# A chained attention, dense MoE and soft MoE kernel: w1 loads on a second queue, later combine steps, working tiles as stream slots, sums turned by pairs

## The chip, the cores and the metric

One core of a Trainium2 chip runs the whole program. The metric is device time in microseconds (us). TensorE is called PE, VectorE DVE, ScalarE ACT, GpSimd POOL, SyncE SP; "idle" of an engine is time between its instructions.

## The reference

Three stages, all float32, with B=4 batches, H=8 heads, S=576, D=64, so N=2304 rows of DM=512:

```
p_packed = softmax(p k^T / 8) v              # 32 packed rows for each head
x   = softmax(q p_packed^T / 8) p_packed     # attention output, 2304 x 512
P   = domain_probs / sum                     # 4 dense experts, F = 1024
x   = sum_e P[:, e] * (relu(x @ w1[e]) @ w2[e])
logits = x @ phi                             # 8 soft experts, 4 slots each: 32 columns
slot_in  = softmax(logits over rows).T @ x   # 32 x 512
slot_out = per expert e: relu(slot_in[e] @ m1[e]) @ m2[e]
out = softmax(logits over columns) @ slot_out
```

w1 and w2 are those of the dense MoE, m1 and m2 those of the soft one (8 x 512 x 1024 and 8 x 1024 x 512).

## The kernel before, in words

**Order of work.** Python emits every engine's instructions in a fixed order, and each engine runs its own list in that order, waiting on semaphores. A head computes attention for batch 0 under a small planner (`place_ops`). Then a loop runs over 128 slots, 32 for each batch. Slot s does `flip_h(s-1)` (a DVE transpose of the hidden block into the ring `hr`), `mm1(s)` (12 matmuls, hidden rows = g x a, L620; ACT, POOL and every fourth half DVE finish them, L630, L631, L625), at every fourth slot `make_g` for the next four slots (L585, L595, L597) and `logits` (L653), and then whatever is due in that slot.

**w1.** `make_g(ci)` multiplies a 1 MB block of w1 by the packed rows. There is one w1 tile, so the load of block ci+1 is issued at the end of `make_g(ci)`, on SP's queue, in SP's list behind all loads emitted before it.

**wphi.** In the head and batch 0 w2 is multiplied by phi (`wphi_ops`): for each of 8 blocks, four PE turns (L260) with ACT copies (L267), a projection (L275), an ACT copy `pick` (L286), a PE turn `back` (L291), an ACT copy `keep` (L294).

**Soft MoE in the loop.** While batch b+1 runs, `softmaxes(b)` is stepped from slots 0 to 3 and at `C_AT`. The latter are the column softmax, here called the combine steps: den and cm (DVE, L735 to L743), a POOL subtraction (L745), an ACT exp (L749), a sum and reciprocal (DVE, L751 to L753), a POOL product (L755), a turn into `cts` (DVE, L758). `pooling(b)` (L775) adds into `tacc`. The attention of the next batch is emitted one stage per slot for group 0 from slot 8 and group 1 from slot 12 (`ATT_AT`); stage 0 turns k (L344), 2 is sa (L358), 3 the maximum (L382), 5 the normalization (L408 to L413), 6 the PE turn `et` (L419), 8 pv (L455), 9 the packing into pkn (L468, L471), 10 sb (L358), 11 nat (L500, L506), 14 the sum (L520), 17 the split of a2 into two parts: `hi` on ACT (L537), `lo` on POOL (L542).

**The stream.** From the last batch on, 80 chunks of 512 KB (16 of w2, 32 of m1, 32 of m2) are loaded on SP in order of use into slots. A slot is a piece of SBUF that has come free: 8 of a pool, 2 of a2, 4 of a ring place, 2 of w1, 4 of g, 2 of a2, 1 of wphi, and 16 of four ring places that become free block by block as the last `pooling` reads them: 39. Chunk 39 goes where chunk 0 was, once that is used. (L849 issues.)

**The end.** After slot 127: last logits, softmax over rows, `pooling` (L775), sums into `tacc` (L789), all remaining combine steps, then 16 turns of `tacc` through `fold` (tt, L1133) with two copies, `si` (L1148, chunks 0 to 15), its turn `sit`, `hid` (L1196, chunks 16 to 47), `so` (L1242, chunks 48 to 79). m2 is taken by four experts at a time: experts 0 to 3 in full width (512), then experts 4 to 7 in two parts of 256 columns, so 16 chunks are in parts. After a part its columns are summed (`sr`, L1259), multiplied by `ct` (o, L1273), copied by ACT and DVE (L1233) and stored (L1280), all before the next part's so on PE.

Of the kernel before, what the change touches and what calls it, by code (L numbers as in the profile page):

```python
# [18 lines left out]
def tile_packed_attention_moe_softmoe(  # L19
# [40 lines left out]
    ATT_AT = (8, 12)  # L60
    C_AT = (8, 9, 10, 11, 12, 13)
# [12 lines left out]
    soft = main.enter_context(tc.tile_pool(name="soft", bufs=1))  # L74
# [39 lines left out]
    flat = [hr[:, i].rearrange("p a b -> p (a b)") for i in range(RING)]  # L114
    m_run = const.tile([128, NB], F32, name="m_run")
# [84 lines left out]
    class Op:  # L200
        def __init__(self, stage, eng, cost, fn, deps, take=0, give=0, rank=0):
# [47 lines left out]
    def wphi_ops(n, loaded, next_load):  # L249
# [48 lines left out]

        puts = []
        for x in range(4):  # L300
            ops.append(Op(0, "PE", 0.47, lambda x=x: turn(x), [loaded], take=1, rank=2))
            ops.append(Op(0, "ACT", 0.58, lambda x=x: put(x), [ops[-1]], give=1, rank=2))
            puts.append(ops[-1])
        ops.append(Op(0, "PE", 1.3, project, puts, take=1, rank=2))
        if next_load:
            next_load.deps.append(ops[-1])
            ops.append(next_load)
        pr = [o for o in ops if o.fn is project]
        ops.append(Op(0, "ACT", 0.27, pick, pr, give=1, rank=2))
        ops.append(Op(0, "PE", 0.15, back, ops[-1:], take=1, rank=2))  # L310
        ops.append(Op(0, "ACT", 0.27, keep, ops[-1:], give=1, rank=2))
# [14 lines left out]
    def attention(b, g, tmp, late, gp, loads=None):  # L326
# [219 lines left out]
    def att_tmp(tag, name):  # L546
        if tag == "a2":
            return sw("t0", name)
# [117 lines left out]
    def sw(tag, name):  # L666
        return soft.tile([128, S], F32, tag=tag, name=name)

    def spread_p(n):

        t = sw("t0", f"ps{n}").rearrange("p (x s) -> p x s", s=32)
# [3 lines left out]
        pe_t[n] = soft.tile([128, S], F32, tag="pe", name=f"pe{n}", bufs=2)  # L675
# [6 lines left out]
    def softmaxes(b, halves=False):  # L682
        la = sw("la", f"la{b}")
# [23 lines left out]
        d = sw("t2", f"d{b}").rearrange("p (x s) -> p x s", s=32)  # L707
# [14 lines left out]
        lt = sw("t1", f"lt{b}").rearrange("p (x s) -> p x s", s=32)  # L722
# [79 lines left out]
    so_steps = [(s, 0, DM) for s in range(NX // 4 - 1)]  # L802
    so_steps += [(NX // 4 - 1, d0, dw) for d0, dw in parts]
# [10 lines left out]
    for s, d0, dw in so_steps:  # L814
        nx = CHUNK // dw
        for x in range(0, NFT, nx):
            for e in range(4):
                chunks.append(
                    m2[4 * s + e, 512 * (x // 4) : 512 * (x // 4) + 512, d0 : d0 + dw].rearrange(
                        "(p x) d -> p x d", x=4  # L820
                    )[:, x % 4 : x % 4 + nx]
                )
# [59 lines left out]
    with tc.manual_schedule():  # L882
# [89 lines left out]
        for n in range(NCH):  # L972
# [7 lines left out]
            ops += wphi_ops(n, landed[n], after)  # L980
            ops.append(Op(0, "NONE", 0.0, done, ops[-1:], rank=2))
        rest = place_ops(ops)
# [57 lines left out]
        for s in range(nslot):  # L1040
# [35 lines left out]
            elif last == SPB - 3:  # L1076
                add_slots(2, w1_place)
            if last >= 0:
# [31 lines left out]
        fin = ctx.enter_context(tc.tile_pool(name="fin", bufs=1, reuse_waits="tile"))  # L1110
        tt = fin.tile([128, 2, NFT, 64], F32, tag="tt", name="tt")
        ct = fin.tile([128, NB // 2, XR, 2, 2, 32], F32, name="ct")
        rr_t = fin.tile([128, DM], F32, name="rr")
# [4 lines left out]
        hm = [fin.tile([128, NFT, 4, 32], F32, name=f"hm{s}") for s in range(2)]  # L1118
        sel = fin.tile([128, 128], F32, name="sel")
        si = leftover(0, DM)  # L1120

        for c in range(4):
            for s in range(2):
                pool.tensor_copy(
                    sel[:, 32 * c + 16 * s : 32 * c + 16 * s + 16].rearrange(
                        "p (x s) -> p x s", x=4
                    ),
                    ident.rearrange("p (x r) -> p x r", x=4)[:, :, 4 * s : 4 * s + 4],
                )
# [12 lines left out]
        ck = 0
        ps = mm_ps("si")
        for x in range(0, NFT, 2):
            cks = [chunk_t.pop(ck + e) for e in range(NE)]
            for xl in range(2):
                for e in range(NE):
                    pe.matmul(  # L1148
                        ps[32 * e : 32 * e + 32, :],
                        tt[:, e % 2, x + xl, 32 * (e // 2) : 32 * (e // 2) + 32],  # L1150
# [22 lines left out]
        for s in range(2):  # L1173
            pool.memset(hm[s], 0.0)
        for s in range(2):
            for dc in range(NDC):
# [5 lines left out]
                )  # L1182

# [23 lines left out]
        hid = fin.tile([128, DF], F32, tag="tt", name="hid")  # L1207
        act.activation(out=hid[:, :512], in_=hp[0], func=AF.Relu)
        dve.tensor_scalar_max(hid[:, 512:], hp[1], 0.0)
        for i in range(2):  # L1210
# [5 lines left out]
            for s in range(2):  # L1216
                (act.copy if i else dve.tensor_copy)(
                    hm[s][:, 4 * i : 4 * i + 4, :, 4 * s : 4 * s + 4].rearrange(
                        "p a b c -> p (a b) c"
                    ),  # L1220
                    ps.rearrange("p (a c) -> p a c", c=32)[:, :, 4 * s : 4 * s + 4],
# [92 lines left out]
```

## Time and profile before

| | us |
|---|---|
| median of 3 runs (lowest, highest) | 508.59 (506.87, 512.04) |
| the profiled execution, its own time | 507.49 |
| its span, first to last instruction | 505.7 |
| PE busy, DVE busy, POOL busy, ACT busy | 472.3, 290.9, 204.4, 181.7 |

The profile is one execution. Its time is its span and 1.8 us around it. Times in the rows count from the span's start. By stage: head to about 58 us, batches 0 to 3 of the loop to about 406 us, the end to 505.7 us. An engine's busy share says little by itself: what counts is what ends last in each stage.

### The profile page before, as it was taken

Reading aid. Unit: us, or ns where it says so; the run is one execution under the profiler, and the core shown is the slowest. Engines: PE = TensorE matmul, PEld = TensorE weight load, DVE = VectorE, ACT = ScalarE, POOL = GpSimd, SP = SyncE. Lnnn points to the kernel's source line nnn. Section 1 sums busy time; section 2 is a strip of 40 time slices with the busy share of each in tenths; the row PEclk is TensorE's granted clock in tenths of the full one; section 3 lists DMA queues with packets and bytes.
Section 4 is the critical chain, followed back from the end, with each engine's and each line's share of the span. In section 5 each row is a group of like instructions: output and inputs, shape, how many; then the busy total and the mean of one; then the engine's idle time right before and its main releaser. Section 6 shows DMA issues by size and latency. Waiting matters only on the chain.

```text
span 505.7 us, 13249 instructions
## 1 busy us (share of the span) xinstructions
PE 472.3 (93%) x5608; PEld 334.9 (66%) x5608; DVE 290.9 (58%) x551; ACT 181.7 (36%) x449; POOL 204.4 (40%) x266
## 2 busy tenths in 40 slices
PE   6899799999999989999998999999999998998695
PEld 3767677778775767778566678775787866322153
DVE  3683355687781777886559588781875545100022
ACT  2475455435440434354224335440434310200033
POOL 3024233357942544586326157941656513100000
PEclk9999999999999999999999899999999997899986
DMA  8989832457231447643215243285672479999997
GB/s 197 382 311 272 298 130 81 135 136 232 84 123 47 131 141 178 177 143 112 86 68 194 71 128 103 86 294 207 244 256 85 166 275 403 414 412 412 383 383 273
DMA packets 57740, 104.36 MB, mean 206 GB/s; under 512 B 5904, under 2 KB 24848, under 8 KB 57680
## 3 DMA queue, kind: packets, MB, share of 16 engines
q1 hardware_dynamic: 57552, 103.36, 59.6%
q8 instruction: 44, 0.72, 0.6%
q0 software_dynamic: 128, 0.15, 0.3%
q14 instruction: 16, 0.13, 0.1%
HBM read 98.78 MB, written 4.72 MB: 205 GB/s over the span
## 4 chain that ended last, share of the span: by engine, by line
PE 77%; DMA 12%; DVE 6%; SPq 3%; ACT 1%; issue 1%; ACTq 0%; DVEq 0%
PE h L620 39%; PE pb L775 8%; PE lg L653 7%; PE g L585 6%; DMA ck<-in_moe_w_dram 4%; DMA hr<-in_moe_w_dram 4%; DMA w<-in_moe_w_dram 4%; PE pv L455 3%; PE sa L358 2%; PE o L1273 2%; SPq L849 2%; PE w2t L260 2%; PE sb L358 2%; PE et L419 1%; PE tt L1133 1%; PE so L1242 1%
## 5 line engine op out<-in xcount | busy, mean ns | idle before, releaser
L631 POOL TENSOR_TENSOR ht<-ht,pe 128x288 f32<-128x288 f32 x192 | 153.1, 807 | 180.0 <-ACT ht L630 179.8
L620 PEld LDWEIGHTS h<-a,g 128*128 128x128 f32 x1536 | 207.2, 188 | 23.2 <-issue 14.7
L620 PE MATMUL h<-a,g 128*128 128x288 f32 x1536 | 222.1, 300 | 0.0
L630 ACT ACTIVATE ht<-h 128x288 f32<-128x288 f32 x192 | 79.0, 412 | 173.6 <-PE h L620 166.3
L641 DVE STREAM_TRANSPOSE hr<-ht 128x576 f32<-128x576 f32 x128 | 97.3, 763 | 45.3 <-POOL ht L631 41.9
L597 DVE TENSOR_TENSOR g<-g,g 128x512 fp32r<-128x512 f32 x64 | 40.9, 679 | 26.2 <-ACT g L595 26.2
L625 DVE SCALAR_TENSOR_TENSOR ht<-h,pe 128x288 f32<-128x288 f32 x64 | 28.0, 438 | 37.5 <-PE h L620 37.5
L595 ACT CAST g<-g 128x512 fp32r<-128x512 f32 x64 | 34.5, 589 | 27.4 <-PE g L585 27.4
L775 PE MATMUL pb<-hr,d 32*32 32x512 f32 x1152 | 40.5, 598 | 0.0
L585 PE MATMUL g<-w,pkn 64*32 64x512 f32 x512 | 36.1, 601 | 2.9 <-DMA w<-in_moe_w_dram 2.8
L653 PE MATMUL lg<-ht,wphi 128*32 128x288 f32 x512 | 38.3, 412 | 0.0
L653 PEld LDWEIGHTS lg<-ht,wphi 128*32 128x32 f32 x512 | 13.5, 109 | 33.2 <-POOL ht L631 22.5
L775 PEld LDWEIGHTS pb<-hr,d 32*32 32x32 f32 x1152 | 18.3, 103 | 14.7 <-issue 10.2
L1233 DVE COPY ob<-o 128x256 f32<-128x256 f32 x12 | 4.7, 422 | 36.5 <-PE o L1273 36.2
L1242 PE MATMUL so<-hr,hm 128*32 128x256 f32 (+1 forms) x136 | 18.0, 455 | 4.7 <-DMA hr<-in_moe_w_dram 4.7
L267 ACT COPY hr<-w2t 128x512 f32<-128x512 f32 x32 | 17.5, 595 | 5.5 <-PE w2t L260 5.4
L260 PE MATMUL w2t<-ident,hr 128*128 128x128 f32 x128 | 18.3, 290 | 0.7 <-ACT pt L286 0.6
L260 PEld LDWEIGHTS w2t<-ident,hr 128*128 128x128 f32 x128 | 15.5, 149 | 3.4 <-issue 0.9
L673 POOL COPY ps<-dpn 128x576 f32<-128x576 f32 x16 | 10.6, 665 | 13.7 <-DVE dpn L195 13.7
L789 DVE SCALAR_TENSOR_TENSOR tacc<-tacc,rsc,pb 128x512 f32<-128x512 f32 x12 | 8.2, 743 | 13.2 <-PE pb L775 13.2
L1242 PEld LDWEIGHTS so<-hr,hm 128*32 128x32 f32 x136 | 6.1, 116 | 14.1 <-DMA hr<-in_moe_w_dram 9.4
L1242 PE MATMUL so<-ck,hm 128*32 128x512 f32 (+1 forms) x52 | 12.3, 531 | 1.1 <-DMA ck<-in_moe_w_dram 1.1
(159 smaller groups left out, 435.4 us busy)
## 6 DMA issues: line engine op xcount, KB each, us to landing
w<-in_moe_w_dram SPq DMA_DIRECT2D x32, 1024.0 KB, 5.2
hr<-in_moe_w_dram SPq DMA_DIRECT2D x40, 512.0 KB, 8.7
ck<-in_moe_w_dram SPq DMA_DIRECT2D x38, 512.0 KB, 8.0
hr<-in_moe_w_dram SPq DMA_DIRECT2D x8, 1024.0 KB, 10.1
k<-in_k_dram SPq DMA_DIRECT2D x16, 288.0 KB, 3.9
v<-in_v_dram SPq DMA_DIRECT2D x18, 192.0 KB, 7.0
q<-in_q_dram SPq DMA_DIRECT2D x12, 288.0 KB, 2.9
out_dram<-ob SPq DMA_DIRECT2D x8, 384.0 KB, 6.0
```

The costliest lines, as they stand in the source:

```text
L260: pe.transpose(st[x][:, 128 * dc : 128 * dc + 128], t[:, x, 128 * dc : 128 * dc + 128], ident,)
L585: pe.matmul(ps[g][c : c + 32, :], pkn_t[b][o : o + 64, g, hp, 0, :], t[o : o + 64, 2 * g + hp, :], start=True, stop=True, tile_position=(o ...
L595: act.copy(gg[:, 0, g], ps[g])
L597: dve.tensor_tensor(out=gg[:, 1, g], in0=ps[g], in1=gg[:, 0, g].bitcast(F32), op=ALU.subtract)
L620: pe.matmul(ps[:, :HS], gg[:, l, g, fs], m[:, ts], start=(g == 0 and i == 0), stop=(g == 1 and i == 2),)
L625: dve.scalar_tensor_tensor(out=ht[:, ts], in0=ps[:, :HS], scalar=0.0, in1=pr[:, ts], op0=ALU.max, op1=ALU.mult,)
L630: act.activation(out=ht[:, ts], in_=ps[:, :HS], func=AF.Relu)
L631: pool.tensor_tensor(out=ht[:, ts], in0=ht[:, ts], in1=pr[:, ts], op=ALU.mult)
L641: dve.transpose(out=hr[:, place(b, i), :, f0 : f0 + 32], in_=ht_t[s].rearrange("p (x t) -> p x t", t=32),)
L653: pe.matmul(lg_t[b][r][32 * x : 32 * x + 32, :HS], wphi[:, NFT * e + 4 * hf + x, :], ht_t[4 * ci + x][:, HS * r : HS * r + HS], start=(ch ...
L775: pe.matmul(pb[c][m : m + 32, :], d[o, x + par, :], hr[o, lo : hi + 1 : hi - lo, x + par, :], start=(x == 0), stop=(x == NBLK - 2), tile_p ...
L1242: pe.matmul(so[32 * e : 32 * e + 32, d0 : d0 + dw], hm[s][:, x + xl, e, :], cks[e][:, dw * xl : dw * xl + dw], start=(s == 0 and x + xl == 0),
```

## The change

- `load_w1`: blocks 1 to 25 are issued from ACT's list (its own queue) in place of SP's; blocks 0 and 26 to 31 stay on SP.
- `wphi_ops`: each block's `back` and `keep` move behind the first two turns of the next block.
- `ATT_AT` goes from (8, 12) to (8, 13); `C_AT` from slots 8 to 13 to 17, 18, 19, 21, 22, 26; `lo` is always on DVE.
- The softmax's working tiles become one constant tile `work`; in the last batch `softmaxes` takes tiles of `ht` instead, and two stream slots are made of `work` (emitted with those of w1 in slot 27 of the last batch in place of slot 29 for w1). The last ring place keeps `ct` and `hm` in place of a pool `fin`, so its four slots go: 37 slots.
- The end: one combine step, 12 idle turns on PE behind `pooling`, then `tacc` is turned by pairs of blocks (4 times 4 matmuls and an ACT copy), each a step ahead of the `si` matmuls that use it; the other combine steps come behind `sit`.
- m2: one expert at a time, experts 0 to 4 in full width, 5 to 7 in parts, so 12 chunks are in parts; successive matmuls of one chunk go to the four column groups of the array, summed by `rep`.

```diff
-    ATT_AT = (8, 12)
-    C_AT = (8, 9, 10, 11, 12, 13)
+    ATT_AT = (8, 13)
+    C_AT = (17, 18, 19, 21, 22, 26)
...
-    soft = main.enter_context(tc.tile_pool(name="soft", bufs=1))
...
+    work = const.tile([128, 6, S], F32, name="work")
...
-        sp.dma_start(
+        (act if 0 < n < (NB - 1) * NCH + 2 else sp).dma_start(
             t, w1[e, :, FC * hf : FC * hf + FC].rearrange("(c p) f -> p c f", p=128)
...
+        pk = add("ACT", 0.27, pick, [pr], 0.5, give=1)
+
+        bk = add("PE", 0.15, back, [pk], 1.15, take=1)
+        kp = add("ACT", 0.27, keep, [bk], 1.15, give=1)
+        add("NONE", 0.0, done, [kp], 1.15)
...
-            (dve if loads else gp).tensor_tensor(out=hl[1], in0=st["a2"], in1=hl[0].bitcast(F32), op=ALU.subtract)
+            dve.tensor_tensor(out=hl[1], in0=st["a2"], in1=hl[0].bitcast(F32), op=ALU.subtract)
...
+            return ht_pool.tile([128, S], F32, tag="ht", name=f"{tag}{b}") if halves else sw(tag)
...
-    so_steps = [(s, 0, DM) for s in range(NX // 4 - 1)]
-    so_steps += [(NX // 4 - 1, d0, dw) for d0, dw in parts]
+    so_steps = [(i, x, 0, DM) for i in range(NX - 3) for x in range(0, NFT, CHUNK // DM)]
+    for d0, dw in parts:
+        so_steps += [
+            (i, x, d0, dw) for i in range(NX - 3, NX) for x in range(0, NFT, CHUNK // dw)
+        ]
...
-        rest = place_ops(ops)
+        rest = sorted(place_ops(ops), key=lambda o: o.key)
...
-            elif last == SPB - 3:
+            elif last == SPB - 5:
                 add_slots(2, w1_place)
+                add_work(0)
+                add_work(1)
...
-        hr_slots([place(b, i) for i in range(NE)])
+        hr_slots([place(b, i) for i in range(NE - 1)])
         fill_stream()
-        for _ in sg[b]:
-            pass
-        main.close()
...
+        next(sg[b])
+        wp = mm_ps("idle")
+        for _ in range(12):
+            pe.transpose(wp[:, :128], ident, ident)
...
+        turn_sums(0)
+        ps = mm_ps("si", keep=True)
         for x in range(0, NFT, 2):
+            if x + 2 < NFT:
+                turn_sums(x // 2 + 1)
...
+            for xl in range(nx):
+                c = (nx * n + xl) % 4
+                pe.matmul(
+                    so[32 * c : 32 * c + 32, d0 : d0 + dw],
+                    hm[:, x + xl, 32 * i : 32 * i + 32],
+                    t[:, dw * xl : dw * xl + dw],
...
-            pe.matmul(sr[:, :dw], sel, so_sb, start=True, stop=True)
+            pe.matmul(sr[:, :dw], rep, so_sb, start=True, stop=True)
```

## Rows read from the trace of the kernel before

**Rows 1.** Busy time by stretch: us, PE, PEld, DVE, ACT, POOL, PE's clock, DMA share, GB/s.

```profile
234.00:330.00 96.00, 93.50 (x1173) 68.74 (x1172) 68.93 (x129) 36.63 (x92) 49.99 (x60) 0.98 0.34 108
330.00:406.00 76.00, 76.00 (x873) 58.18 (x874) 47.24 (x80) 26.89 (x64) 40.62 (x52) 1.00 0.57 208
```

**Rows 2.** PE's waits in 44:60, 60:140, 140:234, 234:330: sum, times, longest.

```profile
PE g L585 <- DMA w<-in_moe_w_dram: 2.5, 1, 2.5
PE wp L291 <- ACT pt L286: 1.2, 2, 0.8
...
PE wp L291 <- ACT pt L286: 1.3, 3, 0.4
...
PE et L419 <- DVE ex L413: 2.2, 1, 2.2
...
PE et L419 <- DVE ex L413: 2.5, 1, 2.5
```

**Rows 3.** Timeline of SP and PE near 45 us: start, us, instruction [idle before].

```profile
40.52 1.09 PE L585 MATMUL g<-w,pkn 64*32 64x512 f32 x16 [0.32 <-DMA w<-in_moe_w_dram]
...
46.34 0.40 SPq L176 DMA_DIRECT2D w<-in_moe_w_dram  x1
...
54.97 1.09 PE L585 MATMUL g<-w,pkn 64*32 64x512 f32 x16 [2.46 <-DMA w<-in_moe_w_dram]
```

**Rows 4.** Busy time by stretch, head, columns as in rows 1.

```profile
46.00:50.00 4.00, 4.00 (x34) 4.00 (x34) 0.78 (x1) 2.58 (x6) 2.43 (x4) 1.00 1.11 223
```

**Rows 5.** Chain of waits, batch 1, slots 11 to 14: start, us, what.

```profile
175.36 0.46 DVE ht L625
...
177.18 0.37 DVE cm L752
...
184.62 0.83 PE et L419 x6
```

**Rows 6.** Busy time by stretch behind batch 2's wait, columns as in rows 1.

```profile
280.00:282.00 2.00, 2.00 (x34) 0.85 (x19) 0.00 (x0) 0.00 (x0) 0.00 (x0) 0.50 0.00 0
```

**Rows 7.** Groups of instructions by line: busy us, mean ns, idle before.

```profile
L743 DVE TENSOR_REDUCE cm<-lt 128x18 f32<-128x576 f32 x4 | 3.0, 747 | 0.0
...
L542 POOL TENSOR_TENSOR a<-a2t,a 128x576 fp32r<-128x576 f32 x6 | 8.6, 1440 | 0.2
...
L542 DVE TENSOR_TENSOR a<-hr,a 128x576 fp32r<-128x576 f32 x2 | 1.5, 758 | 1.0 <-ACT a L537 1.0
```

**Rows 8.** Timelines of DVE and PE in batch 1, slots 21 and 22.

```profile
208.87 0.47 DVE L471 COPY pkn<-pv 32x64 f32<-32x64 f32 x2 [0.31 <-ACT pkn L471]
...
209.59 1.20 PE L358 MATMUL sb<-qt,pkn 32*32 32x288 f32 x32
```

**Rows 9.** Busy time by stretch near the end, columns as in rows 1.

```profile
401.00:405.00 4.00, 4.00 (x32) 4.00 (x32) 2.02 (x3) 1.24 (x3) 1.91 (x4) 1.00 0.29 116
...
426.00:434.00 8.00, 8.00 (x41) 5.34 (x45) 2.66 (x7) 2.68 (x7) 5.03 (x15) 0.55 1.02 418
...
472.00:490.00 18.00, 13.01 (x104) 6.37 (x108) 3.01 (x8) 3.65 (x11) 0.00 (x0) 0.91 1.09 383
```

**Rows 10.** Timelines of SP and PE from 413 us.

```profile
413.29 14.47 SPq L849 DMA_DIRECT2D hr<-in_moe_w_dram  x16
...
422.85 6.98 PE L1133 MATMUL tt<-hr,tacc 128*128 128x64 f32 x32 [2.09 <-DVE den L735]
...
433.42 7.06 SPq L849 DMA_DIRECT2D ck<-in_moe_w_dram  x10
```

**Rows 11.** Chain of waits, the last 26 us: start, us, what.

```profile
480.54 3.24 PE so L1242 x26
...
485.45 1.13 PE o L1273 x10
...
490.00 3.63 PE so L1242 x64
...
500.80 0.42 DVE hr L1233
```

More of the change, by code (lines that the diff above doesn't have):

```diff
@@ L200, in tile_packed_attention_moe_softmoe, with __init__ @@
     class Op:
-        def __init__(self, stage, eng, cost, fn, deps, take=0, give=0, rank=0):
+        def __init__(self, stage, eng, cost, fn, deps, take=0, give=0, rank=0, key=0):
+            self.key = key
             self.stage, self.eng, self.cost, self.fn = stage, eng, cost, fn
@@ L247, in load_w2, with wphi_ops @@
         w2_t[n] = t
-    def wphi_ops(n, loaded, next_load):
+    def wphi_ops(n, loaded, next_load, done):
         st = {}
@@ L297, in keep, with add @@
             let_go([st["ps"]])
+        def add(eng, cost, fn, deps, key, **kw):
+            ops.append(Op(0, eng, cost, fn, deps, rank=2, key=n + key, **kw))
+            return ops[-1]
         puts = []
         for x in range(4):
[L301 to L304, printed above, removed]
+            tr = add("PE", 0.47, lambda x=x: turn(x), [loaded], 0.1 * x, take=1)
+            puts.append(add("ACT", 0.58, lambda x=x: put(x), [tr], 0.1 * x, give=1))
+        pr = add("PE", 1.3, project, puts, 0.5, take=1)
         if next_load:
-            next_load.deps.append(ops[-1])
+            next_load.deps.append(pr)
+            next_load.key = n + 0.5
             ops.append(next_load)
[L308 to L311, printed above, removed]
+        pk = add("ACT", 0.27, pick, [pr], 0.5, give=1)
+        bk = add("PE", 0.15, back, [pk], 1.15, take=1)
+        kp = add("ACT", 0.27, keep, [bk], 1.15, give=1)
+        add("NONE", 0.0, done, [kp], 1.15)
         return ops
@@ L664, in tile_packed_attention_moe_softmoe, with sw @@
     pe_t = {}
-    def sw(tag, name):
-        return soft.tile([128, S], F32, tag=tag, name=name)
+    def sw(tag):
+        return work[:, ("t1", "la", "t2", "t0").index(tag)]
     def spread_p(n):
-        t = sw("t0", f"ps{n}").rearrange("p (x s) -> p x s", s=32)
+        t = sw("t0").rearrange("p (x s) -> p x s", s=32)
         b, e = n // NE, order[n]
@@ L674, in spread_p @@
         yield
-        pe_t[n] = soft.tile([128, S], F32, tag="pe", name=f"pe{n}", bufs=2)
+        pe_t[n] = work[:, 4 + n % 2]
         dve.transpose(out=pe_t[n].rearrange("p (x t) -> p x t", t=32), in_=t)
@@ L813, in tile_packed_attention_moe_softmoe @@
                 chunks.append(m1[4 * s + e, 128 * dc : 128 * dc + 128, :])
[L814 to L822, printed above, removed]
+    for i, x, d0, dw in so_steps:
+        chunks.append(
+            m2[i, 512 * (x // 4) : 512 * (x // 4) + 512, d0 : d0 + dw].rearrange(
+                "(p x) d -> p x d", x=4
+            )[:, x % 4 : x % 4 + CHUNK // dw]
+        )
     chunk_t = {}
@@ L855, in fill_stream, with add_work @@
             limit -= 1
+    def add_work(i):
+        flat_work = work.rearrange("p a b -> p (a b)")
+        add_slots(1, lambda name: flat_work[:, CHUNK * i : CHUNK * i + CHUNK])
     def open_stream(nm, side, spare=0):
@@ L1102, in tile_packed_attention_moe_softmoe @@
         next(pg[b])
-        hr_slots([place(b, i) for i in range(NE)])
+        hr_slots([place(b, i) for i in range(NE - 1)])
         fill_stream()
-        for _ in sg[b]:
-            pass
-        main.close()
[L1110 to L1113, printed above, removed]
+        next(sg[b])
+        wp = mm_ps("idle")
+        for _ in range(12):
+            pe.transpose(wp[:, :128], ident, ident)
+        end = work.rearrange("p a b -> p (a b)")[:, 2 * CHUNK :]
+        tt = end[:, :CHUNK].rearrange("p (x e s) -> p x e s", e=2, s=64)
+        hid = end[:, :CHUNK]
+        own = flat[place(b, NE - 1)]
+        ct = own[:, : NB * S].rearrange(
+            "p (n x b r t) -> p n x b r t", n=NB // 2, x=XR, b=2, r=2
+        )
+        hm = own[:, NB * S :].rearrange("p (x c) -> p x c", x=NFT)
         st2 = [
@@ L1172, in tile_packed_attention_moe_softmoe @@
             pool.memset(st2[dc], 0.0)
-        for s in range(2):
-            pool.memset(hm[s], 0.0)
+        pool.memset(hm, 0.0)
         for s in range(2):
@@ L1182, in tile_packed_attention_moe_softmoe @@
                 )
+        for _ in sg[b]:
+            pass
+        main.close()
         nt = 3
```

101 lines of the change are left out of this document (44 added, 57 removed).

## The prediction

> **What bounds the kernel now.** I read the busy time by stretch first, then PE's waits stretch by stretch, then at each wait the timeline or the chain. The reader is to see that the kernel has two regimes. From about 58 to 406 us PE is the bound: it is busy 93.50 of 96.00 us in batch 2 and all of batch 3's 76.00 [rows 1], so an edit there is worth only the few waits that PE still has, which the rows list in full: 2.5 for a w1 block, 1.2 and 1.3 for `back`, 2.2 and 2.5 for the normalization ahead of `et` [rows 2]. The other engines' long idle times are no gain. From about 413 us the DMA engines are the bound: SP has 16 chunks to issue at once, the DMA share stays at 1.02 to 1.09 [rows 9, 10], and PE waits for chunks, so that a shorter computation between 420 and 460 us buys nothing unless it lets a chunk be loaded sooner. The last 26 us are a chain: so after the last chunk of a part, o, the second part's so, o, store [rows 11].
>
> **Part 1, w1 from ACT's list.** Block 1's matmuls end at 41.6 (40.52 + 1.09), which frees the only w1 tile, but block 2's load is issued at 46.34, behind SP's loads for batch 1, and PE starts on it at 54.97 after 2.46 us idle [rows 3]. So it landed about 8.5 us after its issue. From ACT's list it goes out behind the two ACT casts of `make_g`, about 43, so 3.4 us sooner; with the same 8.5 us it lands at 51.4, before PE arrives at 52.5. Gain 2.5, and 0.3 more at block 1 if that also comes sooner. An ACT issue replaces an SP issue of 0.40 [rows 3]: 25 x 0.4 = 10 us of ACT, whose load is 36.63 of 96 [rows 1] and whose casts come ahead of it. Its wait, that PE has read the old block, is over when the casts run. Queued behind it on ACT are the hidden halves of the next slot, which PE's result banks wait for; PE uses two of six banks for each slot, so 0.4 us is covered. If the cover were gone it would cost 25 x 0.4 = 10. I take a gain of 2.5, bounds 0 and 2.8.
>
> The Trainium skill speaks against this part ("DMA: Bandwidth & Descriptors", Issuing engines are not separate DMA queues): loads issued from several engines run on the same 16 DMA engines and interleave, so that only the sequencer's issue time is saved. The DMA share was already 1.11 when the load waited its turn [rows 4]; if shared engines meant an unchanged landing, the part would give 0, which is the third rival.
>
> **Part 2, `back` later.** PE waits 2.5 us in five places for ACT's `pick` [rows 2]. Two PE turns now stand between, which cover an ACT copy. The last block has no next one, and a part of what stands before 54.97 was hidden in the wait for w1. No instruction is added. I take 1.7, bounds 0.9 and 2.1.
>
> **Part 3, the combine steps and `ATT_AT`.** In batches 1 and 2 the DVE list at slots 11 to 13 holds the combine steps, the maximum, k's turns of group 1 and the normalization in one piece from 175.36 until `et` starts at 184.62 [rows 5]; PE stands still 2.2 and 2.5 us [rows 2]. In batch 2 the clock falls to 0.50 behind it [rows 6]. By that row 1.0 us is lost in its 2 us, and about 1.9 in all (an estimate: batch 2's h and sa at lower clock). So 2.2 + 2.5 + 1.9 = 6.6 can be won. Without cm, its short companions (0.75 + 0.37 [rows 5, 7] and less) and `cts`, and with k's turns of group 1 a slot later, about 3.5 us leave the chain of 9.3 us, more than the 2.5 of wait: this wait goes.
>
> What is late next: the steps come back in slots 17 to 26, beside the second half of both groups. Group 1's sb on PE starts at 209.59, only 0.25 us after DVE has finished pkn (208.87 + 0.47) [rows 8]. Now the sum step (about 0.75 + 0.37 + 0.27 = 1.3, by the cm reduction and the short steps [rows 5, 7]) and, through the shift by one slot, group 0's sum (about 1.2) stand ahead of that packing. What spare time DVE has there takes up about half. I take 1.0 us late at group 1's sb and 0.4 at group 0's, which has den and cm ahead of its packing: 1.4 for each of batches 1 and 2, 2.8 in all. Bounds: none, or as long as before with the clock drop. Group 1's `lo` now comes a slot (1.6 us) later; on DVE it takes 0.76 in place of 1.44 on POOL [rows 7]. Next batch's first h follows about 1 us behind it, so I put this at 0, with a bound of 0.5 for each of three batches. POOL and ACT steps move with the others and have room. Batch 0 has no combine steps, batch 3 no attention. Part 3: 6.6 - 2.8 = 3.8, bounds -1.5 and 6.6.
>
> **Part 4, the stream.** Until 406 us the DMA has room (0.29 [rows 9]) but no free slot. Two slots of `work` are free after slot 26 of the last batch, about 396 us, so two chunks are loaded before the DMA is the bound. A chunk takes 0.524 MB / 418 GB/s = 1.25 us: 2.5 us. The chunks in parts move at 383 GB/s, the others at 418 [rows 9], so 1.37 against 1.25: four fewer of them give 0.5, of which I take 0.4. A part's rows in memory are 1 KB pieces, a full-width chunk's are 4 KB.
>
> Of these 0.4 us the Trainium skill would give nothing: the same page (Specifications) has full rate from 512 bytes on. The row shows otherwise, as far as the width is the cause, and by the page the sum would be 0.4 less.
>
> The four slots less are the danger. Five chunks queued at the loop's end last until about 414, then 12 x 1.25 = 15 us: the DMA runs dry near 429.5 unless chunk 0 to 3 are used by about 427.5. Before, that was at 433.42, after 6.98 us of tt at a clock of about half [rows 9, 10]. Now one pair (a quarter of tt) and a copy stand ahead, and the next pair runs beside the copy. With the 12 idle turns filling most of the idle time from 420.8 to 422.85 I expect full clock: 422.85 + 0.9 + 0.9 + 1.7 for the first si group = 426.4, in time. At half clock it is 429.8, and the DMA loses about 2.5.
>
> **Part 5, the last chain.** The first part's so ended 3.24 us after the last chunk it waited for, as 26 matmuls of that group of four came behind it; now eight do, about 0.9. Then 483.8 to 485.45 for the sum and 4.55 for o stay. The second so has 48 matmuls in place of 64: 3.63 x 48/64 = 2.7 [rows 11]. The last chunk came at about 480.5 + 8 x 1.37 = 491.4; now 2.9 sooner, 488.5, and the last of the first part six chunks before that, 480.3. So: 480.3 + 0.9 + 1.65 + 4.55 + 2.7 = 490.1 in place of 493.6, a gain of 3.5 in parts 4 and 5 together. The rest, from 493.6 to the end, keeps its length; the stores of the first part follow the loads in the queue and end just as the second part's begin, so there is no more to be had. Moving the combine steps, `ct` and the zeroing of `hm` costs nothing: they run while hid keeps PE busy. Bounds of 4 and 5: 0.5 (dry, half clock) and 4.7.
>
> **Sum.** 2.5 + 1.7 + 3.8 + 3.5 = 11.5. Against the profiled execution's own 507.5 this gives 496.0. The median of the runs, 508.6, is 1.1 higher, so I predict 497.1.
>
> **Rivals.** (a) DVE is late again: the waits of batches 1 and 2 come back at sb, with the clock drop, and part 3 gives 0: 500.9. For it: 0.25 us of margin; against it: DVE has idle time between those slots. (b) The stream runs dry or PE stays at half clock behind `pooling`, so that parts 4 and 5 give 0.5: 500.1. For it: four slots less, and a clock that fell in just this place; against it: the 12 turns. (c) Block 2 of w1 lands no sooner: 499.6. For it the full DMA; against it, that it would no longer stand behind SP's list. (d) Slower: ACT is held at its 25 issues. SP's list shows that an issue can wait for room, 14.47 us for 16 chunks, 0.9 each [rows 10]. ACT would hold the next slot's halves, and PE waits once ACT is later than the banks cover, one to two slots (1.6 to 3.3 us). From 11.5/25 = 0.5 us of lost PE time for each issue it eats all; held for 3 us, over a cover of 2, it costs 25 x 1.0 = 25: 522. Against it: in the loop the DMA share is 0.34 [rows 1]. (e) The change does not do what it says, for example one tile `work` makes its users wait for each other: then the waits stay and only the end is won, 505.
>
> **Chances.** Forecast 0.50, (a) 0.18, (b) 0.14, (c) 0.06, (d) 0.06, (e) 0.06. The range: best 2.8 + 2.1 + 6.6 + 4.7 = 16.2, thus 492.4; the upper end takes in (a) with (b), 497.1 + 3.8 + 3.0 = 503.9, and a little of what the bounds of part 3 leave, 504.5. A change of less than 1%, about what a measurement of this kernel can tell from none, is 503.5 to 513.7. Faster by over that 0.82, within 0.12, slower 0.06.
>
> **What would show it.** Right: no wait of PE for w near 50 us; no `back` wait but the last; no wait at `et` in batches 1 and 2, a short one at sb; batch 2 as long as batch 1; clock 1.00 from 420 to 434; no dip of the DMA share near 430; the last so about 3.5 us sooner from the loop's end. Wrong: PE waiting for ACT behind its DMA issues, sb waits over 2 us, half clock or a dip in the DMA at 425 to 435, or a next batch's h waiting for `lo`.

## The result and the profile after

The median is 501.22 us (500.28 to 504.44) against 508.43 us of the kernel before (506.87 to 512.04) on the same chip: ratio 0.985, 95% interval 0.9807 to 0.9894. The change is faster by 7.2 us; 497.1 was predicted, with a range of 492.4 to 504.5. The sign and the range held; 4 us of the forecast gain are missing.

The profiled execution of after took 500.28 us (span 498.5). Four marks divide it: in the chain of waits, the matmuls `lr` sum up a batch's logits of the soft MoE, one row for each batch. Chain of waits of after (start, us, what):

```profile
138.98 0.97 PE lr L701 x4
...
231.39 0.97 PE lr L701 x4
...
324.07 0.97 PE lr L701 x4
...
400.42 1.30 PE lr L701 x4
```

The same rows of before stand at 141.86, 235.48, 331.19 and 407.54, its span ends at 505.7.

| stretch | before | after | gain | predicted |
|---|---|---|---|---|
| start to the first `lr` (parts 1, 2) | 141.86 | 138.98 | 2.88 | 4.2 |
| to the second | 93.62 | 92.41 | 1.21 | 3.8 in |
| to the third | 95.71 | 92.68 | 3.03 | both |
| to the fourth | 76.35 | 76.35 | 0.00 | 0 |
| to the end (parts 4, 5) | 98.16 | 98.08 | 0.08 | 3.5 |

So the loop gave 4.24, a little more than forecast, the head 1.3 too little, and the end nothing. Each column is one profiled execution.

**Loop.** PE's waits of after in 44:60, 60:140, 140:234 and 234:330 (sum, times, longest), which answer to [rows 2]:

```profile
PE pw L277 <- ACT hr L269: 1.5, 1, 1.5
...
PE wp L293 <- ACT pt L288: 0.4, 1, 0.4
PE h L627 <- DVE a L549: 0.2, 1, 0.2
...
PE h L627 <- DVE a L549: 0.2, 1, 0.2
...
PE h L627 <- DVE a L549: 0.2, 1, 0.2
```

The waits for w, for `back` (one short one is left) and at `et` are gone. New are 0.2 us ahead of a batch's first h, and 1.5 us for ACT near 45 us. The matmuls sb, 1.13 us each in before's chain of waits, last longer; the first of batch 2 in after's chain:

```profile
284.26 1.72 PE sb L365 x32
```

**Head.** Timeline of after near 45 us, which answers to [rows 3] (in brackets: idle time before, and what ended it):

```profile
43.81 0.39 ACTq L177 DMA_DIRECT2D w<-in_moe_w_dram  x1
...
44.56 0.27 ACT L296 COPY wphi<-wp 128x128 f32<-128x128 f32 x1 [2.17 <-DMA k<-in_k_dram]
...
45.37 1.06 PE L277 MATMUL pw<-hr,tacc 128*32 128x128 f32 x26 [1.48 <-ACT hr L269]
...
53.13 1.09 PE L592 MATMUL g<-w,pkn 64*32 64x512 f32 x16
```

Block 2 of w1 leaves 2.5 us sooner than in before and no longer delays g. But ACT stood still for 2.17 us around that issue, and PE waited 1.48 us for the weights ACT had yet to copy. The profile puts ACT's stop down to a load of k. The trace has ACT's own wait ahead of the issue, though, and it is for a load of p: SP issued that one at 36.30, it landed at 43.73, and the w1 load, which uses the same completion semaphore next, left ACT at 43.81. In all seven kernels that issue block 2 from ACT the issue follows that landing by 0.07 or 0.08 us.

The two heads also differ in PE's clock, here in 10:20, before and then after (columns as in [rows 1]):

```profile
10.00:20.00 10.00, 7.44 (x90) 4.96 (x83) 7.79 (x21) 3.56 (x13) 0.57 (x1) 1.00 1.08 330
...
10.00:20.00 10.00, 7.60 (x96) 5.91 (x89) 7.65 (x20) 4.47 (x15) 0.67 (x1) 0.71 1.08 333
```

The first g starts at 26.9 us in before and at 26.6 in after all the same. What the lower clock cost ahead of it was not tried. From the first g to the last of the first three w1 blocks both stand at full clock, and there after gains 1.6 us.

**Loop and end by stretch** (us, PE, PEld, DVE, ACT, POOL, PE's clock, DMA share, GB/s), which answer to [rows 1, 9]; the first two lines are batches 1 and 2:

```profile
137.20:229.60 92.40, 92.20 (x1169) 67.84 (x1169) 68.04 (x127) 37.57 (x94) 48.10 (x58) 1.00 0.43 132
229.60:322.30 92.70, 92.48 (x1170) 67.81 (x1169) 70.25 (x130) 36.72 (x93) 48.14 (x58) 1.00 0.34 112
418.00:420.00 2.00, 2.00 (x19) 0.61 (x11) 0.00 (x0) 0.28 (x1) 0.00 (x0) 1.00 1.02 416
426.00:428.00 2.00, 1.32 (x16) 0.13 (x4) 0.56 (x1) 0.00 (x0) 0.00 (x0) 1.00 1.02 418
432.00:434.00 2.00, 2.00 (x16) 0.51 (x12) 1.05 (x3) 1.73 (x4) 0.13 (x1) 0.51 1.02 404
466.00:468.00 2.00, 0.98 (x16) 0.16 (x8) 0.00 (x0) 0.00 (x0) 0.00 (x0) 1.00 1.09 380
472.00:474.00 2.00, 1.08 (x8) 0.20 (x8) 0.00 (x0) 0.33 (x1) 0.00 (x0) 0.50 1.09 368
480.00:482.00 2.00, 2.00 (x15) 1.44 (x11) 0.95 (x3) 1.08 (x4) 0.00 (x0) 0.50 1.05 358
484.00:486.00 2.00, 2.00 (x32) 1.04 (x28) 0.00 (x0) 0.00 (x0) 0.00 (x0) 0.71 1.00 349
486.00:488.00 2.00, 1.21 (x14) 0.33 (x6) 0.00 (x0) 0.62 (x2) 0.00 (x0) 1.00 0.18 61
```

PE is busy all but 0.2 us of a batch. Behind `pooling` the clock is full until 430 us (0.55 in [rows 9]), and the DMA share stays above 1.0, also while the clock is at half between 430 and 434 us: the stream doesn't run dry. Then m2 begins, one expert at a time: PE works half of each stretch (0.98 of 2.00 at 466 us), waiting for chunk after chunk, and from 472 us it is granted half its clock (0.50, the lower of its two levels, 1.2 GHz) until about 485 us. At 486 us the DMA is idle while PE still has work ahead: the stream no longer sets the end.

PE's waits of after in 460:500:

```profile
PE so L1269 <- DMA hr<-in_moe_w_dram: 4.3, 8, 0.8
```

Chain of waits of after, the last 26 us, which answers to [rows 11]:

```profile
472.52 1.13 PE so L1269 x8
...
475.79 6.63 PE o L1298 x36
482.43 4.14 PE so L1269 x48
...
489.34 3.08 PE o L1298 x20
```

The eight matmuls behind the first part's last chunk begin 72.1 us after `lr` (73.0 in before), but o takes 6.63 us and the second so 4.14, where 4.55 and 2.7 were forecast.

### The profile page after: what moved, and what is told of

Read it like the earlier page. It is cut to its first block, busy times and chain, and to the rows that moved or that the text cites. A ratio compares the mean times of both kernels' runs of the same rounds, so it can differ in the third digit from the quotient of the medians.

```text
span 498.5 us, 13271 instructions
## 1 busy us (share of the span) xinstructions
PE 471.6 (95%) x5604; PEld 329.7 (66%) x5604; DVE 295.4 (59%) x556; ACT 182.9 (37%) x452; POOL 198.0 (40%) x251
## 4 chain that ended last, share of the span: by engine, by line
PE 69%; DMA 16%; DVE 8%; ACT 2%; SPq 2%; POOL 1%; issue 1%; DVEq 0%; ACTq 0%
PE h L627 35%; PE pb L788 8%; PE lg L660 6%; PE g L592 6%; DMA w<-in_moe_w_dram 4%; DMA hr<-in_moe_w_dram 4%; DMA ck<-in_moe_w_dram 4%; PE o L1298 2%; DMA work<-in_moe_w_dram 2%; PE pv L462 2%; DMA k<-in_k_dram 2%; PE sb L365 2%; PE w2t L262 2%; DVE hr L648 2%; DVE g L604 1%; DMA hr<-in_v_dram 1%
## 5 line engine op out<-in xcount | busy, mean ns | idle before, releaser
L638 POOL TENSOR_TENSOR ht<-ht,work 128x288 f32<-128x288 f32 x192 | 155.2, 818 | 176.2 <-ACT ht L637 175.9
L627 PE MATMUL h<-a,g 128*128 128x288 f32 x1536 | 224.5, 300 | 0.6 <-DVE a L549 0.6
L632 DVE SCALAR_TENSOR_TENSOR ht<-h,work 128x288 f32<-128x288 f32 x64 | 28.1, 439 | 23.1 <-PE h L627 22.8
L592 PE MATMUL g<-w,pkn 64*32 64x512 f32 x512 | 34.9, 601 | 2.4 <-DMA w<-in_moe_w_dram 1.6
L788 PE MATMUL pb<-hr,work 32*32 32x512 f32 x864 | 30.6, 598 | 0.0
L788 PEld LDWEIGHTS pb<-hr,work 32*32 32x32 f32 x864 | 12.6, 103 | 11.4 <-issue 8.7
L1269 PE MATMUL so<-hr 128*32 128x256 f32 (+1 forms) x84 | 12.6, 511 | 4.9 <-DMA hr<-in_moe_w_dram 4.7
L680 POOL COPY work<-dpn 128x576 f32<-128x576 f32 x16 | 10.9, 680 | 13.5 <-DVE dpn L196 13.5
L1269 PE MATMUL so<-ck,hr 128*32 128x256 f32 (+1 forms) x80 | 12.2, 550 | 1.1 <-DMA ck<-in_moe_w_dram 1.1
L683 DVE STREAM_TRANSPOSE work<-work 128x576 f32<-128x576 f32 x16 | 12.2, 763 | 0.0
## 6 DMA issues: line engine op xcount, KB each, us to landing
hr<-in_moe_w_dram SPq DMA_DIRECT2D x8, 1024.0 KB, 10.1
```

Source lines behind the costliest of these rows:

```text
L592: pe.matmul(ps[g][c : c + 32, :], pkn_t[b][o : o + 64, g, hp, 0, :], t[o : o + 64, 2 * g + hp, :], start=True, stop=True, tile_position=(o ...
L627: pe.matmul(ps[:, :HS], gg[:, l, g, fs], m[:, ts], start=(g == 0 and i == 0), stop=(g == 1 and i == 2),)
L632: dve.scalar_tensor_tensor(out=ht[:, ts], in0=ps[:, :HS], scalar=0.0, in1=pr[:, ts], op0=ALU.max, op1=ALU.mult,)
L638: pool.tensor_tensor(out=ht[:, ts], in0=ht[:, ts], in1=pr[:, ts], op=ALU.mult)
L788: pe.matmul(pb[c][m : m + 32, :], d[o, x + par, :], hr[o, lo : hi + 1 : hi - lo, x + par, :], start=(x == 0), stop=(x == NBLK - 2), tile_p ...
L1269: pe.matmul(so[32 * c : 32 * c + 32, d0 : d0 + dw], hm[:, x + xl, 32 * i : 32 * i + 32], t[:, dw * xl : dw * xl + dw], start=(nx * n + xl ...
```

## The experiments

Theory A, formed from these rows: the end lost its gain because the one-expert order leaves PE half idle ahead of o, so that it stands at half clock through o and the second so; and the head lost some because ACT is held at its issue of block 2. The rivals: the end is set by the stream or by the new order itself, whatever the clock; the head by when the full DMA lands block 2, whichever engine issues it. For each kernel three measures: the median with its ratio to before on the same chip; the time from the fourth `lr` to the end; and, in the head, from the first to the last matmul g of the first three w1 blocks ("g to g"). That one is read from the line of g (fastest, median and slowest in ns, then the first and the last start); in after, 53.6 less 26.6:

```profile
L592 PE MATMUL g<-w,pkn x48: 586/589/615, 26.6 to 53.6; 64*32 64x512 f32 x48
```


| kernel | median us | ratio, 95% interval | `lr` to end | g to g |
|---|---|---|---|---|
| before | 508.4 | | 98.2 | 28.6 |
| after | 501.22 | 0.985 (0.9807 to 0.9894) | 98.1 | 27.0 |
| e1_busy_so | 497.24 | 0.9785 (0.9748 to 0.9822) | 93.9 | 27.8 |
| e2_w1_on_sp | 502.73 | 0.9876 (0.9843 to 0.9909) | 98.9 | 27.3 |
| e3_before_steps | 505.21 | 0.9913 (0.9881 to 0.9945) | 97.7 | 29.3 |
| e4_no_work_slots | 506.03 | 0.9939 (0.9907 to 0.9972) | 101.3 | 29.0 |
| e5_m2_by_fours | 498.81 | 0.9814 (0.9779 to 0.9849) | 95.0 | 27.4 |
| e6_no_idle_turns | 503.16 | 0.9897 (0.9851 to 0.9944) | 100.7 | 26.5 |
| e8_block2_pool | 499.5 | 0.9823 (0.9773 to 0.9873) | 98.0 | 25.3 |
| e9_lo_pool | 503.65 | 0.991 (0.9877 to 0.9942) | 98.1 | 27.6 |
| e10_fill_and_pool | 494.84 | 0.9753 (0.9699 to 0.9807) | 94.2 | 25.4 |
| e11_back_early | 502.97 | 0.9897 (0.9865 to 0.9929) | 97.5 | 29.2 |
| e12_fill_more | 495.49 | 0.9761 (0.9718 to 0.9803) | 95.2 | 25.5 |

The kernels ran on several chips, so ratios are compared, not medians. Against after, the intervals of e4 and e12 stand clear and that of e10 touches; the others overlap, and what they show is read from the stretches of one profiled execution each. Kernels that share after's end (e2, e8, e9, e11) took 97.5 to 98.9 from `lr` to the end, so a difference there under 1.4 us says little.

### e1_busy_so: PE kept busy behind the chunks of m2's first part

```diff
+        wp = mm_ps("idle")
...
             load_chunk()
+            if dw < DM and d0 == 0:
+                for _ in range(6):
+                    pe.transpose(wp[:, :128], ident, ident)
```

> The changed kernel with six idle turns on PE behind each of the six chunks of m2's first part, nothing else. Theory A (the end lost its gain to the clock: PE at 0.50 from 472 to 485 us, o of the first part 6.63 us in place of 4.55, the second so 4.14 in place of 2.7, and 0.7 around the sum): the clock stays at 1.00, o takes about 4.55 again and the time falls by 3.5 to 4.2 us, to about 497. Rival B (the end is bound by the bytes of loads and stores): the last store ends where it did, change under 1 us. Rival C (the turns stand in the way of the chunks' matmuls): 1 to 2 us slower.

Busy time by stretch of e1 (columns as above):

```profile
472.00:474.00 2.00, 2.00 (x26) 1.15 (x24) 0.00 (x0) 0.00 (x0) 0.00 (x0) 1.00 1.09 385
480.00:482.00 2.00, 2.00 (x34) 1.15 (x35) 0.81 (x3) 0.60 (x2) 0.00 (x0) 1.00 1.10 364
```

Its chain of waits:

```profile
473.01 0.81 PE idle L1282 x6
473.82 0.57 PE so L1270 x8
...
476.10 1.13 PE o L1302 x10
...
477.25 3.39 PE o L1302 x22
480.64 2.77 PE so L1270 x48
```

The only edit is work that nobody reads, and the end is 4.1 us shorter. The clock is 1.00, o takes 4.52 (1.13 + 3.39), so 2.77: the two durations that the prediction had used. The last so ends 81.6 us after `lr` (483.42 less 401.85); the prediction's 490.1 less 407.54 is 82.6. Theory A holds for the end.

### e5_m2_by_fours: m2 four experts at a time again

```diff
-    so_steps = [(i, x, 0, DM) for i in range(NX - 3) for x in range(0, NFT, CHUNK // DM)]
+    so_steps = [(i, x, 0, DM) for x in range(0, NFT, CHUNK // DM) for i in range(4)]
...
-        so_steps += [
-            (i, x, d0, dw) for i in range(NX - 3, NX) for x in range(0, NFT, CHUNK // dw)
-        ]
+        so_steps += [(i, x, d0, dw) for x in range(0, NFT, CHUNK // dw) for i in range(4, NX)]
```

with the chunks of four experts taken together.

> The changed kernel with m2 taken by four experts at a time again, in the new layout (16 chunks in parts, each group's matmuls in the order of before). Theory A: the matmuls come in dense bursts again, the clock is back at 1.00 when the first part's o starts, o takes about 4.6 us; against that the first part's so ends 3.2 us after its last chunk and two more chunks follow it, so the time is within 1 us of the changed kernel's. Rival B (bound by bytes): 0.5 us slower by the four chunks more in parts. Rival D (the new order of m2 is the gain of the end, the clock is nothing): 3 us slower.

Busy time by stretch of e5:

```profile
466.00:468.00 2.00, 2.00 (x20) 0.96 (x24) 0.00 (x0) 0.00 (x0) 0.00 (x0) 0.50 1.07 371
470.00:472.00 2.00, 1.21 (x14) 0.55 (x18) 0.00 (x0) 0.00 (x0) 0.00 (x0) 1.00 1.09 386
```

The row of its chain of waits that answers to after's 472.52:

```profile
471.41 1.93 PE so L1267 x26
```

Its end is 3.1 us shorter than after's (95.0 against 98.1), its median 2.4 lower with overlapping intervals; a time within 1 us of after's was expected. The half clock comes here too, but earlier (466 to 470 us), while chunks are still to come, and the clock is full again when the last group's matmuls and o begin. So the order of m2 costs by where it puts the half clock; the longer piece behind the last chunk (1.93 against 1.13) is the smaller price.

### e2_w1_on_sp and e8_block2_pool: who issues w1

```diff
-        (act if 0 < n < (NB - 1) * NCH + 2 else sp).dma_start(
+        sp.dma_start(
```

> The changed kernel with all w1 loads on SP again. Theory A (on ACT the second load waits for an older load's landing, holds ACT 2.2 us and PE 1.5, so that the queue is worth only about 1 us): PE's wait for block 2 near 50 us comes back with about 2.4 us, the hold of ACT goes, time 0.5 to 1.5 us longer. Rival F (the queue is worth the 2.5 us of the wait): 2.5 us longer. Rival G (ACT's issues cost more than they give): shorter.

```diff
-        (act if 0 < n < (NB - 1) * NCH + 2 else sp).dma_start(
+        (pool if n == 2 else act if 0 < n < (NB - 1) * NCH + 2 else sp).dma_start(
```

> The changed kernel, with the load of w1's block 2 issued by POOL and all later ones by ACT as before. Theory H (ACT is held at its issue of block 2 until an earlier load has landed, and PE waits 1.48 us for hr from ACT): POOL is idle there and can stand; PE's wait for hr goes, block 2 lands as early, 0.8 to 1.5 us sooner: about 500. Rival (the full DMA sets when p, wphi and block 2 land, whoever issues): PE waits as long for w or hr near 45 to 53 us, 501 to 502.

The end of block 1's g, the issue of block 2 and the g that uses it in e2 (timeline):

```profile
40.04 1.09 PE L592 MATMUL g<-w,pkn 64*32 64x512 f32 x16 [0.60 <-DMA w<-in_moe_w_dram]
...
45.74 0.40 SPq L177 DMA_DIRECT2D w<-in_moe_w_dram  x1
...
53.51 1.09 PE L592 MATMUL g<-w,pkn 64*32 64x512 f32 x16 [2.31 <-DMA w<-in_moe_w_dram]
```

The same in e8:

```profile
40.98 1.09 PE L592 MATMUL g<-w,pkn 64*32 64x512 f32 x16
...
43.01 0.83 POOL L177 DMA_DIRECT2D w<-in_moe_w_dram  x1
...
43.10 0.28 ACT L296 COPY wphi<-wp 128x128 f32<-128x128 f32 x1
...
52.47 1.09 PE L592 MATMUL g<-w,pkn 64*32 64x512 f32 x16 [0.34 <-DMA w<-in_moe_w_dram]
```

On SP the wait for w is back (2.31). On POOL ACT goes on without a stop and PE waits 0.34. The heads differ ahead of this stretch (e8's first g starts at 27.7 us, e2's at 26.7, with PE's clock at 0.65 in 20:30 in e8), which is why g to g is used, and why the load is timed from the end of block 1's g (41.13 in e2, 42.07 in e8, 41.25 in after):

| block 2 of w1 | issued behind block 1's g | took to land | landed behind block 1's g |
|---|---|---|---|
| e2, from SP | 4.6 | 7.6 | 12.2 |
| after, from ACT | 2.6 | 8.7 | 11.3 |
| e8, from POOL | 0.9 | 9.3 | 10.3 |

So the load leaves 3.7 us sooner from POOL than from SP but takes longer, and lands 2.0 sooner. g to g it is 27.3 on SP, 25.3 on POOL (25.4 and 25.5 in e10, e12), and 26.5 to 29.0, mean 27.6, in after, e1, e4, e5, e6 and e9, which leave the issue on ACT and have the same head: from POOL the sooner landing is worth 2.0 us, and on ACT nothing of it is left on the mean. ACT's stop does that in two ways: it holds the issue, and it holds the copies that PE needs. In e1 and e9 PE then waits 0.3 and 0.8 us for the load as well. SP's side rests on one execution, and by the ratios after is still 1.3 us faster than e2, with overlapping intervals. e8's median is 1.7 below after's; the intervals overlap there too, so this rests on the stretch.

### e3_before_steps: the kernel before with part 3 alone

```diff
-    ATT_AT = (8, 12)
-    C_AT = (8, 9, 10, 11, 12, 13)
+    ATT_AT = (8, 13)
+    C_AT = (17, 18, 19, 21, 22, 26)
...
-            (dve if loads else gp).tensor_tensor(out=hl[1], in0=st["a2"], in1=hl[0].bitcast(F32), op=ALU.subtract)
+            dve.tensor_tensor(out=hl[1], in0=st["a2"], in1=hl[0].bitcast(F32), op=ALU.subtract)
```

> The kernel before with the later combine steps, group 1 of attention a slot later and the split of a2 on DVE, nothing else. Theory A (the loop's gain is this part): batches 1 and 2 get shorter by 1.2 and 3.0 us as in the changed kernel, 504.2 in place of 508.4. Rival E (the freed w1 queue or the tile of its own also matters for the loop): a gain under 2 us.

From `lr` to `lr` batches 1 and 2 take 92.41 and 92.65 us, as in after: the whole gain of the loop is part 3's. The head of its profiled execution ran at a clock of 0.78 in 0:14 and 0.61 in 14:28, which its span carries.

### e9_lo_pool: `lo` back on POOL

```diff
-            dve.tensor_tensor(out=hl[1], in0=st["a2"], in1=hl[0].bitcast(F32), op=ALU.subtract)
+            (dve if loads else gp).tensor_tensor(out=hl[1], in0=st["a2"], in1=hl[0].bitcast(F32), op=ALU.subtract)
```

> The changed kernel with the step lo back on POOL (1.44 us an instruction) in place of DVE (0.76). It comes last in a batch, and the next batch's first h needs it: PE waits 0.2 us there three times in the changed kernel. If the step stands on that path: three waits of 0.5 to 1 us more, 502.5 to 504. If POOL begins it sooner than a busy DVE can: no change, 501.2.

PE's waits in 140:234:

```profile
PE h L627 <- POOL a L549: 0.9, 1, 0.9
```

The 0.2 us ahead of the next batch's h become 0.9, three times. The median is 2.4 above after's, of which these waits show 2.1; the intervals overlap, so this rests on the waits. By them `lo` had to go to DVE with the later slot.

### e11_back_early: part 2 undone

```diff
-        bk = add("PE", 0.15, back, [pk], 1.15, take=1)
-        kp = add("ACT", 0.27, keep, [bk], 1.15, give=1)
-        add("NONE", 0.0, done, [kp], 1.15)
+        bk = add("PE", 0.15, back, [pk], 0.55, take=1)
+        kp = add("ACT", 0.27, keep, [bk], 0.55, give=1)
+        add("NONE", 0.0, done, [kp], 0.55)
```

> The changed kernel with back and keep of a block ahead of the next block's turns again, as in the kernel before. By part 2 of the prediction PE waits again for ACT's pick in four places between 14 and 60 us, 1.7 us together (2.1 at most): 503. Rival: what PE loses there it gets back at its later waits for ACT and for w (the DMA sets the pace of the head): within 0.5 us of the changed kernel.

PE's waits in 44:60 and 60:140:

```profile
PE wp L293 <- ACT pt L288: 0.9, 2, 0.4
...
PE wp L293 <- ACT pt L288: 1.3, 3, 0.4
```

2.2 us of waits in place of 0.4, and a median 1.75 higher, with overlapping intervals. In this profile PE's clock also falls, to 0.61 in 48:52, where after has 1.00, so not all of the 2.2 us that g to g is longer is the waits. Nothing later gives it back.

### e4_no_work_slots and e6_no_idle_turns: the stream and the clock behind `pooling`

```diff
                 add_slots(2, w1_place)
-                add_work(0)
-                add_work(1)
```

> The changed kernel without the two chunk slots in the tile work, so that two chunks fewer are loaded ahead of the loop's end. Theory S (the stream of chunks sets the end, each chunk 1.25 us of DMA): the first part's last chunk lands 2.5 us later and the time is 2.5 longer, about 503.7. Rival C (PE at half clock behind the chunks sets the end and the DMA has time in hand): within 0.8 of the changed kernel, 501 to 502.

```diff
-        wp = mm_ps("idle")
-        for _ in range(12):
-            pe.transpose(wp[:, :128], ident, ident)
```

(the 12 behind `pooling`)

> The changed kernel without the 12 idle turns of PE behind pooling. If they hold the clock up through pooling and tt (the condition of rival b of the prediction): the clock falls to half near 420 us, tt and the first si take about 1.7 us longer, the DMA runs dry near 430 us, and the time is 1.5 to 3 us longer: 503 to 504. If the order by pairs alone had done it: no lower clock at 418 to 430, DMA share at 1.0 or more throughout, 501 to 501.5.

PE's longest wait of e4 in 40:60:

```profile
PE pw L277 <- ACT hr L269: 2.6, 1, 2.6
```

ACT's longest wait there:

```profile
ACT wphi L296 <- DMA k<-in_k_dram: 3.3, 1, 3.3
```

Its chain of waits at the first part's last chunk:

```profile
477.77 1.13 PE so L1267 x8
```

The matmuls behind the first part's last chunk begin 75.3 us after `lr` (477.77 less 402.47) in place of 72.1, and the end is 3.2 longer: theory S, which put 2.5 on the two chunks; where the other 0.7 comes from is open. The other 2 us of its loss are in the head, where ACT happened to be held for 3.3 us and PE's clock was 0.50 in 46:48 behind its wait.

e6, busy time by stretch:

```profile
418.00:420.00 2.00, 2.00 (x11) 0.81 (x14) 0.00 (x0) 0.37 (x1) 0.00 (x0) 0.50 1.03 420
424.00:426.00 2.00, 2.00 (x20) 1.31 (x20) 0.00 (x0) 0.37 (x1) 0.00 (x0) 1.00 0.92 307
```

Half clock at tt, then the DMA down to 307 GB/s, as rival b has it, and 2.6 us more from `lr` to the end. Rival b was a real danger, and the 12 turns are what kept it off.

### e10_fill_and_pool and e12_fill_more: the versions that beat both

e10 is e1's and e8's edits together; e12 adds four idle turns each ahead of sr and of o, in both parts:

```diff
+            w2p = mm_ps("idle")
             sr = mm_ps(f"sr{d0}")
+            for _ in range(4):
+                pe.transpose(w2p[:, :128], ident, ident)
             pe.matmul(sr[:, :dw], rep, so_sb, start=True, stop=True)
+            for _ in range(4):
+                pe.transpose(w2p[:, :128], ident, ident)
```

> The changed kernel with six idle PE turns behind each chunk of m2's first part and w1's block 2 issued by POOL. If both gains hold and stand in different stretches, they add: 4.0 by the first edit and 0.8 to 1.5 by the second, 495.7 to 496.5. If the load gains nothing: 497.2, as with the idle turns alone.

> The changed kernel with both edits of the combination (six idle turns behind each chunk of m2's first part, block 2 of w1 issued by POOL), and four idle turns each ahead of sr and of o in both parts, where PE waits for ACT 0.49 and 0.47 us. The combination took 494.84, and its clock fell to 0.65 and 0.50 in the last o, whose second piece took 4.45 us in place of 3.39 at full clock. If those idle stretches brought the clock down, 0.8 to 1.2 us less: 493.8. If o by itself brings it down: the same as the combination, or 0.2 more.

e10 took 494.84 us: 25.4 g to g and 94.2 from `lr` to the end, both gains in one kernel. In its last o the clock falls (0.65 in 484:486). In e12 it does not, as this stretch shows:

```profile
484.00:486.00 2.00, 1.98 (x20) 1.26 (x17) 1.20 (x4) 1.21 (x4) 0.00 (x0) 1.00 0.47 164
```

Chain of waits of e12:

```profile
482.06 0.59 PE idle L1290 x4
...
484.88 3.08 PE o L1307 x20
```

The last o piece takes 3.08 against 4.45, so the short idle stretches ahead of it had their part in the fall, as far as one execution of each shows. The time is not better (495.49; the intervals overlap). From the last so's end to the span's end it is 12.0 us in e12 and 12.3 in e10: what o won was nearly all waited for behind it, at the stores. e12's so also ended 1.3 us later after `lr` than e10's. By the timelines 0.9 of that stands ahead of its own idle turns (the first part's last matmuls begin 73.1 us after `lr`, in e10 72.2), and 0.4 between them and o, where the turns are.

## Why the prediction was right, and where a term was off

The time alone says little for it: 501.2 is nearer to rivals (a), 500.9, and (b), 500.1, than to 497.1, and parts 4 and 5 gave 0.08, under their own bound of 0.5. That the sum stayed within its range is owed to the width of the other bounds, and so to luck. The mechanism is borne out, or not, by the rows, part by part.

- **Part 1 (2.5).** Its direction is right: sooner issue, sooner landing, no wait for w; worth 2.0 by POOL against SP. "With the same 8.5 us" did not hold: the load took 8.5 to 10.1 us from POOL (9.3 in e8) and 7.9 to 10.1 from ACT, so that e8's 3.7 us at the issue became 2.0 at the landing. Rival c, the full DMA, so has a share of the loss. The 1.11 of [rows 4] that the prediction put beside it is the DMA share of 46:50, when the load was under way; in 42:46, while it waited its turn, it was 0.83. The Trainium skill ("DMA: Bandwidth & Descriptors", Issuing engines are not separate DMA queues) has loads of several engines interleave on the same DMA engines, and another issuing engine save the sequencer's time alone. These rows agree: the saving is the wait in SP's list, and the longer time to land, which fits the interleaving, takes part of it back. What failed is the sentence that ACT's wait "is over when the casts run": in the seven kernels ACT stood 1.9 to 3.3 us, the issue included, until another load had landed. Rival d named that danger, but spread it over 25 issues at 0.5 us or more; in 60 to 406 us ACT waited for no DMA at all. It was one issue, in the stretch where the DMA is full.
- **Part 2 (1.7).** Right: 1.8 of waits went by e11, and undoing it costs 1.75, part of it perhaps by the clock. Parts 1 and 2 together gave 2.9 in place of 4.2. With the issue on POOL g to g is 1.5 to 1.7 us shorter still, which is more than the missing 1.3; the lower clock ahead of the first g may have a part in it too.
- **Part 3 (3.8).** Right at 4.24. Both waits at `et` (2.2, 2.5) and the half clock of [rows 6] are gone. The loss behind it was seen in the right place, at sb, but not as a wait: the rows of sb in the chain last 1.46 and 1.38 in batch 1, 1.72 and 1.38 in batch 2, in place of 1.13, 1.4 us together where 2.8 was put. What else batch 1 lost (2.2 won, 1.21 gained, 0.6 of it at sb) is 0.2 ahead of h and small shifts. The margin of [rows 8] was enough, so rival a did not come. `lo` was taken at 0 with a bound of 0.5 each: 0.2.
- **Part 4 (stream).** Right. The first part's last chunk is used 72.1 us after `lr`, where the prediction's 480.3 is 72.8. The two early chunks count (e4) and the stream stays full only because PE's clock does (e6). Turning the sums by pairs was not tried by itself, nor were the four column groups of m2.
- **Part 5 (last chain).** This is the term that was mis-sized: "1.65 + 4.55 + 2.7" behind 0.9 for eight matmuls, 9.8 us. It took 14.05 (472.52 to 486.57). The edit was costed by matmul counts at full clock. [Rows 9] had the clock at 0.91 in this stretch already (0.50 in 482:484, back at 1.00 before o's larger piece), but the prediction asked what half clock would do to tt alone. Chunks taken one by one spread the same matmuls thinly over the loads, and the clock fell just ahead of the only piece there that PE sets. The 4.25 us lost are the 3.5 of parts 4 and 5, the 0.7 that the stream came sooner than forecast, and rounding; behind so, 11.9 us are left against 12.1 before. With the clock held (e1) the end gains 4.2.
- **Chances.** Rival (c)'s 499.6 is faster than 503.5, so by the prediction's own bounds its 0.06 belongs to "faster": 0.88 in place of 0.82, and 0.06 for "within".

The Trainium skill describes a pattern like that of part 5 ("TensorE: Matmul & The Clock Gate", HAM oscillation): bursts of matmuls shorter than the load they wait for leave PE throttled. These rows agree in what came of it, but the Trainium skill's case waits 3 to 5 us behind each burst, and here bursts of 0.64 us stood between waits of 0.7 to 0.8. By the Trainium skill's formula on the same page (Terms: throttled time times the clock's missing share) an estimate is 12 us at 0.50 and 2 at 0.71, 6.6 us lost. e1 measured 4.1: o took 6.63 us in place of 4.52, 1.5 times as long and not twice.

## What to carry to other kernels

Cost the piece behind the last transfer at the clock PE will have there: if the order ahead of it makes PE wait chunk by chunk, put idle turns into those waits. Before moving a load to another engine's list, ask what that engine does next, who waits for it, and which older load has to land before the issue can leave; here POOL, which was idle, issued it without loss. Time a load from what frees its place, not from the span's start, when two heads differ. Undoing one part at a time and comparing stretches between fixed marks separated terms of 2 us that the medians alone could not.

## What the hardware showed that was not expected

- Being busy did not bring the clock back by itself: in 476 to 482 us of after PE is recorded busy 2.00 of 2.00 with o (32x128 weights) and stays at 0.50; with so's matmuls (128x32 weights, from 482.43) it is 0.50 in 482:484, 0.71 in 484:486 and 1.00 in 486:488. Not every o is slow: after's last one ran at 1.00 from 488 to 492 us.
- A load's issue can hold ACT although the place it writes is free: 1.9 to 3.3 us at one issue near 43 us with the DMA share at 1.03 (40:50), none in the loop. In seven traces the issue leaves 0.07 or 0.08 us behind the landing of the load, issued by SP 7 to 9 us earlier, that had the same completion semaphore; a kernel with other semaphores was not tried.
- Matmuls that nobody reads made the kernel 4 us faster.
